# Four raw weight tiles loaded among the first attention blocks, converted beside the second to fifth, with every clamp on VectorE

## The chip, the cores and the metric

The kernel runs on one core of a Trainium2 chip. The metric is the device time of one launch in microseconds (us). The engines are TensorE (PE, matrix products into PSUM), VectorE (DVE), ScalarE (ACT), GpSimd (POOL) and SyncE (SP), which here issues all DMA transfers. Each engine works through its own list of instructions in order; semaphores tie the lists together.

## The reference

Everything is 32-bit floating point. Attention with two kinds of mask feeds a gated layer, and this feeds a layer that takes the largest of three products.

```python
batch, n_heads, seq, head_dim = (4, 8, 576, 64)
scores = scale * np.matmul(q, k.transpose(0, 1, 3, 2))
mask_local = (rel >= 0) & (rel < stride)                 # heads 0 to 3, stride 32
mask_strided = (rel >= 0) & (pos[None, :] % stride == pos[:, None] % stride)   # heads 4 to 7
...                                                      # softmax over the last axis
x = np.ascontiguousarray(attn_out.transpose(0, 2, 1, 3)).reshape(B * S, H * D)   # 2304 x 512
g = x @ w_gate                                           # 512 x 1536
silu = g * (1.0 / (1.0 + np.exp(-g)))
x = silu * (x @ w_val) @ w_out                           # 512 x 1536, then 1536 x 512
h = np.maximum(np.maximum(x @ w1, x @ w2), x @ w3)       # 512 x 768 each
return h @ w_out2                                        # 768 x 512
```

The weights reach the core as 64-bit words (a tile of 128 x 512 weights is 512 KB) and are converted there.

## The kernel before

**Two halves.** In the first half, attention and the gated layer run together, over five chunks of at most 480 of the 2304 tokens (`ROWS`). For each chunk there are 12 slots, one for each 128 columns of the hidden layer: gate product and SiLU (`emit_gate`, L499), value product and multiplication by the SiLU (`emit_val`, L507; the multiplication is L511 on DVE), and output product one slot later (`emit_out`, L517). In the second half the three products of the last layer and their maximum run for three pairs of token blocks (`Group`, `out2`).

**Split numbers.** Each operand of a product is split into a high and a low part (`split`, L122: the high part is a copy on ACT, L126, the low part a subtraction on DVE or POOL, L129), and each product is three matmuls: high with high (L484), high with low (L485), low with high (L486).

**Weights.** `load` (L136) brings a raw tile of 64-bit words into one of four buffers (`raw_p`). `convert` (L141) turns it into 32-bit numbers: `q` from the low words (L149 on POOL for the first three tiles, else L151 on ACT), the absolute value of the high words (L152, ACT), a clamp of it (L154, DVE, but POOL for the first three tiles), then shift and mask (L156), merge of the sign (L157) and sum with `q` (L158), all on DVE. `split_w` (L161) splits the result. The order of the 36 tiles is gate 0, value 0, gate 1, value 1, output 0, gate 2, value 2, output 1 and so on (L686). In the first chunk the kernel makes three weight steps in each slot (L716: load up to three tiles ahead, convert one, split one); before it stand eight such steps (`LEADW`).

**Early attention.** The first chunk can't begin before its part of `x` is there. Eight blocks (four strided ones, four local ones, each a pair of units) are loaded ahead of all else, in order (L730); after the blocks whose number is in `RAW_AT` one raw weight tile is put into the queue. The loop at L735 then runs scores (L286, PE), masked maximum (L294, DVE), exponentials (L299, ACT), normalization (L304), transposes (L309) and their copy (L312 or L314), the product with V (L323) and the split into `xh` and `xl` (L328 ACT, L329 DVE); the last three run four blocks later than the first ones. In this loop `step_cvt()` converts weight tiles.

**Order on the engines.** The program is written in one order and a scheduler, with a cost model of its own, makes the order on each engine from it when the kernel is built. The attention of the other chunks is made in pieces (`fill`, L772) in the slots of the chunk before; it uses L397 and L419 (POOL products), L400 and L422 (DVE sums) and more local blocks. The conversion of the second half's weights is tied to the slots from the second chunk on (L774 to L781).

Of the kernel before, what the change touches and what calls it, by code (L numbers as in the profile page):

```python
# [12 lines left out]
ALU = mybir.AluOpType  # L13
# [32 lines left out]

NRING = 4
SEAM = 9
RAW_AT = [2, 7]
SCALE = 1.0 / D ** 0.5  # L50
MASKED = -1.0e9 / SCALE

W_MIN = 2.0 ** -15
W_MAX = 122879.9921875
# [3 lines left out]
def tile_attention_swiglu_maxout(  # L58
# [11 lines left out]
    nc = tc.nc  # L70
# [29 lines left out]
    def f32(ap):  # L100
        return ap.bitcast(F32)
# [39 lines left out]
    def convert(key):  # L141

        raw = raws.pop(key)
        hi, lo = raw[:, :, 1], raw[:, :, 0]
        q = wpool.tile([128, 512], I32, name="q", tag="w")
        w = wpool.tile([128, 512], I32, name="w32", tag="w")

        if n_cvt[0] < 3 and key[0] in ("g", "v", "o"):
            nc.gpsimd.tensor_scalar(q, lo.bitcast(U32), 2.0 ** -29, 1.0, ALU.mult, ALU.mult)  # L149
        else:  # L150
            nc.scalar.activation(q, lo.bitcast(U32), AF.Copy, scale=2.0 ** -29)  # L151
        nc.scalar.activation(f32(w), f32(hi), AF.Abs)  # L152
        eng = nc.gpsimd if key[0] in ("g", "v", "o") and n_cvt[0] < 3 else nc.vector
        eng.tensor_scalar(f32(w), f32(w), W_MIN, W_MAX, ALU.max, ALU.min)  # L154

        nc.vector.tensor_scalar(w, w, 3, 0x3FFFFFFF, ALU.logical_shift_left, ALU.bitwise_and)  # L156
        nc.vector.scalar_tensor_tensor(w, hi, -0x40000000, w, ALU.bitwise_and, ALU.bitwise_or)  # L157
        nc.vector.tensor_tensor(w, w, q, ALU.add)  # L158
        cvt[key] = f32(w)
# [171 lines left out]
    def local_block(g, early=False):  # L331


        def dst(src):
            for c, i0, i1, o in pieces(LR * g[0], LR * (g[-1] + 1)):
                t, w = slice(i0 * STRIDE, i1 * STRIDE), slice(o * STRIDE, (o + i1 - i0) * STRIDE)
                xh, xl = x_tile(c)
                yield xh[:, 0:2, t], xl[:, 0:2, t], src[:, :, w]

        return Block(loc[g[0]:g[-1] + 1], KB, [mask[0 if n % (NI // LR) == 0 else 1] for n in g], dst, early)  # L340

    def strided_block(srcs, b, g, early=False):

        _, rows, nr = ON_PE[b]

        def dst(src):
            for u, n in enumerate(g):
                r0 = min(n * nr, STRIDE - nr)
                su = src[:, :, u * QB:u * QB + nr * rows].rearrange("p a (r i) -> p a r i", i=rows)
                for c, i0, i1, o in pieces(b * NI, b * NI + rows):  # L350
                    def part(t):
                        t = t[:, 2:4, :width(c)].rearrange("p a (i r) -> p a r i", r=STRIDE)
                        return t[:, :, r0:r0 + nr, i0:i1]

                    xh, xl = x_tile(c)
                    yield part(xh), part(xl), su[:, :, :, o:o + i1 - i0]

        return Block(srcs[g[0]:g[-1] + 1], rows * nr, [smask[b]] * len(g), dst, early)

    def pairs(ns):  # L360
        ns = list(ns)
        return [ns[i:i + 2] for i in range(0, len(ns), 2)]
# [329 lines left out]
    n_load, n_cvt, n_split = [0], [0], [0]  # L692
# [6 lines left out]
    def step_load(upto):  # L699
        while n_load[0] < min(upto, limit[0]):  # L700
            key = order[n_load[0]]
            load(key, source(key))
            n_load[0] += 1
# [12 lines left out]
    def weight_step():  # L716
        step_load(n_cvt[0] + AHEAD)
        step_cvt()
        step_split(nc.gpsimd)
# [6 lines left out]
    if True:  # L726
        blocks = [strided_block(st0, 0, g, True) for g in pairs(range(st0.shape[0]))]
        blocks += [local_block(g, True) for g in pairs(range(EARLY))]
        nc.sync.dma_start(cst, shape_consts)
        for i, blk in enumerate(blocks):  # L730
            blk.load()
            if i in RAW_AT:
                step_load(n_load[0] + 1)
        lag = 4
        for i in range(len(blocks) + lag):  # L735
            if i < len(blocks):
                blocks[i].scores()
                blocks[i].softmax(nc.gpsimd if i % 3 == 2 else nc.vector)
            if len(blocks) - 2 <= i < len(blocks):
                step_cvt()  # L740
            if i >= lag:
                blocks[i - lag].transpose(nc.vector if i % 3 == 2 else nc.scalar)
                blocks[i - lag].pv()
        step_split(nc.gpsimd)
        step_split(nc.gpsimd)
        step_load(n_cvt[0] + 2)
        step_cvt()
        for k in range(LEADW):
            weight_step()
        pending = None  # L750
        slots = [(c, f) for c in range(NC) for f in range(NF)]
        fill = {}
        for c in range(1, NC):
            for i, st in enumerate(attention_steps(c)):
                fill.setdefault(i if c == 1 else (c - 1) * NF + i - 3, []).extend(st)
        later = [step for g in range(NFP) for i in range(3) for step in pair_steps(i, g)]
        later += [step for f in range(NF2) for step in wo2_steps(f)]
        due, done = 0.0, 0
        for s, (c, f) in enumerate(slots):
            work = c == 0  # L760
            if c > 0:
                reload("v", f)
                reload("o", f)
            if work:
                weight_step()
            t = emit_gate(c, f)
            if work:
                weight_step()
            emit_val(c, f, t)
            if work:  # L770
                weight_step()
            for step in fill.get(s, []):  # L772
                step()
            if c > 0:  # L774
                due += PACE[c]
                with ExitStack() as tied:
                    for ins in last_val:
                        tied.enter_context(tc.issue_after(ins))
                    while later and done < int(due):
                        later.pop(0)()  # L780
                        done += 1  # L781
            if (c, f) == (NC - 1, SEAM):
                assert not later
                attn.close()
                two = ctx.enter_context(ExitStack())
                y_p, yr0_p = (sub(two, n, 1, side="right", reuse_waits="tile") for n in ("y", "yr0"))
                ring0_p = sub(two, "ring0", 1, side="right", reuse_waits="tile")
                yr_p = [yr0_p]
                ring_p = [ring0_p]
                y = [split_y(load_y(0, k)) for k in range(2)]  # L790
                load_w(0, 0, 0)
            if pending is not None:
                emit_out(*pending)
            pending = (c, f)
        emit_out(*pending)
# [130 lines left out]
```

## Time and profile before

| | before |
|---|---|
| median of three runs | 881.88 us (879.77 to 882.62) |
| profiled execution | 881.39 us, of which span 879.6 us |
| PE busy | 820.3 us (93%) |
| DVE busy | 555.9 us (63%) |
| ACT busy | 384.0 us (44%) |
| POOL busy | 382.3 us (43%) |

The span is what the trace covers, from the first instruction to the last. Shares are means over stages that are limited by different things; in 40 slices of 22 us each, in tenths, the page gives:

```text
PE   5789879898999989999998889999999999999997
DVE  2988999967757598668768943433545254433441
```

PE is the engine that works nearly all the time in the later slices, DVE in slices two to eight (22 to 176 us).

### The profile page before, as it was taken

Reading aid. Unit: us, or ns where it says so; the run is one execution under the profiler, and the core shown is the slowest. Engines: PE = TensorE matmul, PEld = TensorE weight load, DVE = VectorE, ACT = ScalarE, POOL = GpSimd, SP = SyncE. Lnnn points to the kernel's source line nnn. Section 1 sums busy time; section 2 is a strip of 40 time slices with the busy share of each in tenths; the row PEclk is TensorE's granted clock in tenths of the full one; section 3 lists DMA queues with packets and bytes.
Section 4 is the critical chain, followed back from the end, with each engine's and each line's share of the span. In section 5 each row is a group of like instructions: output and inputs, shape, how many; then the busy total and the mean of one; then the engine's idle time right before and its main releaser. Section 6 shows DMA issues by size and latency. Waiting matters only on the chain.

```text
span 879.6 us, 12559 instructions
## 1 busy us (share of the span) xinstructions
PE 820.3 (93%) x4376; PEld 731.7 (83%) x4376; DVE 555.9 (63%) x1097; ACT 384.0 (44%) x857; POOL 382.3 (43%) x301
## 2 busy tenths in 40 slices
PE   5789879898999989999998889999999999999997
PEld 5677658687788878999897779989999899989986
DVE  2988999967757598668768943433545254433441
ACT  4778586734445454364634233432335123422221
POOL 0443654474757676667596632430213021211110
PEclk9789789999999999999999989999999999999999
DMA  9868757896695759869676687578856476453601
GB/s 234 244 219 289 235 187 260 320 366 189 209 330 192 245 190 312 275 207 319 208 249 234 224 268 225 189 245 342 330 217 213 182 251 245 175 215 118 241 1 72
DMA packets 81774, 203.76 MB, mean 232 GB/s; under 512 B 9484, under 2 KB 50224, under 8 KB 78128
## 3 DMA queue, kind: packets, MB, share of 16 engines
q1 hardware_dynamic: 81712, 202.97, 68.1%
q8 instruction: 35, 0.57, 0.2%
q14 instruction: 27, 0.22, 0.1%
HBM read 161.26 MB, written 41.68 MB: 231 GB/s over the span
## 4 chain that ended last, share of the span: by engine, by line
PE 49%; DVE 10%; DMA 4%; ACT 4%; issue 3%; POOL 2%; SPq 0%; DVEq 0%; ACTq 0%; POOLq 0%
PE ps_a L585 13%; PE ps_z L658 8%; PE ps_c L585 6%; PE ps_b L585 3%; PE ps_v L484 2%; PE ps_g L484 2%; PE ps_v L485 2%; PE ps_v L486 2%; PE ps_g L486 2%; PE ps_g L485 2%; PE ps_y L484 2%; PE ps_y L486 2%; PE ps_y L485 2%; DVE w L156 2%; DMA w_v<-wvdr 1%
## 5 line engine op out<-in xcount | busy, mean ns | idle before, releaser
L129 POOL TENSOR_TENSOR hl<-t,hh 128x384 fp32r<-128x384 f32 x36 | 37.6, 1048 | 208.5 <-ACT hh L126 167.2
L484 PE MATMUL ps_g<-xh,wh_g 128*128 128x448 f32 (+1 forms) x240 | 94.4, 393 | 10.4 <-ACT ht L504 8.1
L129 POOL TENSOR_TENSOR hl<-ht,hh 128x448 fp32r<-128x448 f32 (+1 forms) x60 | 75.5, 1258 | 60.5 <-ACT hh L126 58.8
L419 POOL TENSOR_TENSOR pr<-stv,stsc 128x1088 f32<-128x1088 f32 (+17 forms) x44 | 75.2, 1710 | 58.1 <-DVE sto L422 35.9
L486 PE MATMUL ps_v<-xh,w_v 128*128 128x448 f32 (+1 forms) x240 | 91.5, 381 | 8.2 <-DVE w_v L129 8.2
L484 PE MATMUL ps_v<-xh,w_v 128*128 128x448 f32 (+1 forms) x240 | 92.4, 385 | 4.4 <-ACT w_v L126 2.4
L585 PE MATMUL ps_a<-yhT,wr 128*128 128x384 f32 x324 | 94.4, 338 | 0.6 <-ACT s L599 0.6
L486 PE MATMUL ps_g<-xh,wl_g 128*128 128x448 f32 (+1 forms) x240 | 92.7, 386 | 1.3 <-POOL wl_g L129 1.3
L485 PE MATMUL ps_g<-xl,wh_g 128*128 128x448 f32 (+1 forms) x240 | 92.4, 385 | 0.0
L485 PE MATMUL ps_v<-xl,w_v 128*128 128x448 f32 (+1 forms) x240 | 91.1, 379 | 0.0
L485 PE MATMUL ps_y<-hl,w_o 128*128 128x448 f32 (+1 forms) x240 | 89.2, 376 | 1.0 <-POOL hl L129 1.0
L397 POOL TENSOR_TENSOR pr<-stk,stq 128x1088 f32<-128x1088 f32 (+17 forms) x44 | 76.9, 1747 | 30.1 <-DVE stsc L400 23.2
L486 PE MATMUL ps_y<-hh,w_o 128*128 128x448 f32 (+1 forms) x240 | 86.4, 377 | 2.3 <-POOL w_o L129 2.3
L484 PE MATMUL ps_y<-hh,w_o 128*128 128x448 f32 (+1 forms) x240 | 86.2, 380 | 0.2 <-ACT w_o L126 0.2
L599 ACT ACTIVATE s<-ps_a 128x384 f32<-128x384 f32 x81 | 39.4, 490 | 98.4 <-PE ps_a L585 98.1
L126 ACT ACTIVATE hh<-ht 128x448 fp32r<-128x448 f32 (+1 forms) x60 | 35.2, 587 | 106.0 <-DVE ht L511 105.6
L658 PE MATMUL ps_z<-wo2t,hh 128*128 128x512 f32 x216 | 64.8, 392 | 0.9 <-ACT osb L667 0.7
L484 PEld LDWEIGHTS ps_g<-xh,wh_g 128*128 128x128 f32 x240 | 47.2, 197 | 19.1 <-ACT ht L504 10.5
L511 DVE TENSOR_TENSOR ht<-ps_v,ht 128x448 f32<-128x448 f32 (+1 forms) x60 | 37.8, 630 | 37.9 <-PE ps_v L486 26.6
L585 PEld LDWEIGHTS ps_a<-yhT,wr 128*128 128x128 f32 x324 | 59.7, 188 | 1.7 <-ACT s L599 1.1
L486 PEld LDWEIGHTS ps_v<-xh,w_v 128*128 128x128 f32 x240 | 46.1, 192 | 15.1 <-DVE w_v L129 10.3
L484 PEld LDWEIGHTS ps_v<-xh,w_v 128*128 128x128 f32 x240 | 46.2, 192 | 11.1 <-DVE ht L511 3.4
(134 smaller groups left out, 1971.5 us busy)
## 6 DMA issues: line engine op xcount, KB each, us to landing
wr<-wsdr SPq DMA_DIRECT2D x27, 1792.0 KB, 7.2
raw<-in_w_dram SPq DMA_DIRECT2D x60, 512.0 KB, 4.8
w_v<-wvdr SPq DMA_DIRECT2D x48, 512.0 KB, 5.0
w_o<-wodr SPq DMA_DIRECT2D x48, 512.0 KB, 4.9
wsdr<-whi SPq DMA_DIRECT2D x27, 256.0 KB, 3.3
wvdr<-w_v SPq DMA_DIRECT2D x12, 512.0 KB, 4.1
wodr<-w_o SPq DMA_DIRECT2D x12, 512.0 KB, 5.2
loct<-in_loc_dram SPq DMA_DIRECT2D x24, 192.0 KB, 6.5
```

What stands on the lines that cost most here:

```text
L126: a = nc.scalar.activation(hi, src, AF.Copy)
L129: return a.ins, lo_eng.tensor_tensor(lo, src, f32(hi), ALU.subtract).ins
L156: nc.vector.tensor_scalar(w, w, 3, 0x3FFFFFFF, ALU.logical_shift_left, ALU.bitwise_and)
L397: eng.tensor_tensor(pv, self.k[:, 0:i + 1, :], self.q[:, r:r + 1, :].to_broadcast([128, i + 1, D]), ALU.mult)
L419: eng.tensor_tensor(pv, self.v[:, :, 0:i + 1], self.sc[:, r:r + 1, 0:i + 1].to_broadcast([128, D, i + 1]), ALU.mult)
L484: nc.tensor.matmul(ps, wh, xh, start=first, stop=False)
L485: nc.tensor.matmul(ps, wh, xl, start=False, stop=False)
L486: nc.tensor.matmul(ps, wl, xh, start=False, stop=last)
L511: m = nc.vector.tensor_tensor(t, ps[:, :n], t, ALU.mult).ins
L585: nc.tensor.matmul(ps, wts[:, c, a, ks], y[k][b], start=first and k == q == 0, stop=k == 1 and q == 2, skip_group_check=True,)
L599: nc.scalar.activation(s, self.a, AF.Copy)
L658: nc.tensor.matmul(z[j], a[:, ts], w[:, f, b], start=f == q == 0, stop=f == NF2 - 1 and q == 2)
```

## The change

Four raw tiles instead of two go into the queue among the eight blocks' loads: after the blocks 0, 1, 3 and 5 instead of 2 and 7. The early loop converts four tiles, in its steps 1 to 4, instead of two in its steps 6 and 7. After the loop nothing else is taken out, so that the program then stands two conversions further on. The clamp of the first three tiles moves from POOL to DVE; their `q` stays on POOL.

```diff
-RAW_AT = [2, 7]
+RAW_AT = [0, 1, 3, 5]
...
-        eng = nc.gpsimd if key[0] in ("g", "v", "o") and n_cvt[0] < 3 else nc.vector
-        eng.tensor_scalar(f32(w), f32(w), W_MIN, W_MAX, ALU.max, ALU.min)
+        nc.vector.tensor_scalar(f32(w), f32(w), W_MIN, W_MAX, ALU.max, ALU.min)
...
                 blocks[i].scores()
                 blocks[i].softmax(nc.gpsimd if i % 3 == 2 else nc.vector)
-            if len(blocks) - 2 <= i < len(blocks):
+            if 1 <= i < 5:
                 step_cvt()
```

Since one line is gone, every line behind it has a number lower by one in the changed kernel (L152 stays, L156 becomes L155, L312 becomes L311).

The order on ACT at the program's start, before: exponentials of the first four blocks (`sme`, 128x64), copy of the first transposed block (`qe`), exponentials of the fifth (128x96), and the first absolute value of a raw tile (`w_384` is gate 0).

```order
L299 ACT_TABLE_LOAD
L299 ACTIVATE sme,state<-sme,state 128x64 x16
L312 ACTIVATE qe<-ps_a 64x512
L299 ACTIVATE sme,state<-sme,state 128x96 x4
L328 ACTIVATE xh<-ps_a 128x2x4x15
L299 ACTIVATE sme,state<-sme,state 128x96 x4
L328 ACTIVATE xh<-ps_a 128x2x4
L152 ACTIVATE w_384<-raw 128x512
```

The same place now (`w_253`, `w_278`, `w_303` and `w_328` are gate 0, value 0, gate 1 and value 1).

```order
L152 ACTIVATE w_253<-raw 128x512
L298 ACTIVATE sme,state<-sme,state 128x64 x4
L152 ACTIVATE w_278<-raw 128x512
L298 ACTIVATE sme,state<-sme,state 128x64 x4
L152 ACTIVATE w_303<-raw 128x512
L298 ACTIVATE sme,state<-sme,state 128x64 x8
L151 ACTIVATE q<-raw 128x512
L152 ACTIVATE w_328<-raw 128x512
L311 ACTIVATE qe<-ps_a 64x512
L298 ACTIVATE sme,state<-sme,state 128x96 x4
```

The work on the four raw tiles now stands in front of the exponentials of the first, the second and the third block and of the copy of the first transposed block; before, the first of it stood behind the exponentials of the sixth block.

The order on DVE before, at the last piece of `xl` that the first gate product needs (128x2x96; `w_545` and `w_557` are gate 1 and value 1).

```order
L329 TENSOR_TENSOR xl<-ps_a,xh 128x2x128
L329 TENSOR_TENSOR xl<-ps_a,xh 128x2x4
L157 SCALAR_TENSOR_TENSOR w_545<-raw,w_545 128x512
L157 SCALAR_TENSOR_TENSOR w_557<-raw,w_557 128x512
L329 TENSOR_TENSOR xl<-ps_a,xh 128x2x96
```

The same place now (`w_591`, `w_605` and `w_619` are value 2, output 1 and gate 3, the seventh to ninth tile; the last row is the last piece of `xl` of the first chunk).

```order
L155 TENSOR_SCALAR w_605<-w_605 128x512
L153 TENSOR_SCALAR w_619<-w_619 128x512
L328 TENSOR_TENSOR xl<-ps_a,xh 128x2x128
L328 TENSOR_TENSOR xl<-ps_a,xh 128x2x96
L156 SCALAR_TENSOR_TENSOR w_591<-raw,w_591 128x512
L156 SCALAR_TENSOR_TENSOR w_605<-raw,w_605 128x512
L301 TENSOR_SCALAR stat<-stat 128x4
L155 TENSOR_SCALAR w_619<-w_619 128x512
L328 TENSOR_TENSOR xl<-ps_a,xh 128x2x4x15
```

The first gate product's last input now stands behind work on the ninth weight tile; before, behind work on the fourth.

## Rows read from the trace of the kernel before

**Rows 1.** Busy time by stage: us, then PE, PEld, DVE, ACT, POOL, granted clock, DMA.

```profile
0.00:52.10 52.10, 35.32 (x272) 30.93 (x272) 32.96 (x162) 32.67 (x125) 14.70 (x17) 0.90 0.81 225
52.10:156.30 104.20, 92.38 (x467) 74.79 (x467) 100.93 (x187) 74.44 (x154) 52.77 (x35) 0.90 0.75 245
156.30:179.30 23.00, 19.44 (x102) 15.42 (x102) 22.86 (x38) 15.40 (x31) 11.86 (x10) 0.93 0.92 335
179.30:245.00 65.70, 60.97 (x335) 50.79 (x334) 46.73 (x91) 27.14 (x66) 45.81 (x33) 0.97 0.74 255
19.99:40.63 20.64, 15.73 (x190) 13.41 (x190) 19.03 (x87) 16.15 (x64) 11.00 (x9) 0.86 0.92 257
24.75:41.90 17.15, 12.25 (x140) 10.60 (x141) 16.27 (x63) 12.46 (x49) 9.73 (x7) 0.79 0.80 236
```

**Rows 2.** PE's waits from 42 to 220 us: total, times, longest.

```profile
PE ps_v L486 <- DVE w_v L129: 8.2, 6, 2.9
PE ps_a L309 <- POOL sm L304: 3.2, 2, 2.4
```

**Rows 3.** DVE's groups from 80 to 180 us.

```profile
L157 DVE SCALAR_TENSOR_TENSOR w<-raw,w 128x512 int32<-128x512 int32 x23 | 22.8, 990 | 0.1
L158 DVE CUSTOM_DVE_ANT_0 w<-w,q 128x1024 uint16<-128x1024 uint16 x23 | 20.6, 896 | 0.1
L154 DVE TENSOR_SCALAR w<-w 128x512 f32<-128x512 f32 x23 | 16.5, 719 | 0.0
L156 DVE TENSOR_SCALAR w<-w 128x512 int32<-128x512 int32 x23 | 15.7, 685 | 0.2
```

**Rows 4.** PE's order of time: scores of blocks 2, 3 and 5; first gate product.

```profile
9.98 1.97 PE L286 MATMUL ps_a<-ke,qe 128*128 128x64 f32 x8 [0.94 <-DMA ke<-in_st_dram]
14.76 1.94 PE L286 MATMUL ps_a<-ke,qe 128*128 128x64 f32 x8 [2.81 <-DMA ke<-in_st_dram]
...
19.74 1.71 PE L286 MATMUL ps_a<-ke,qe 128*128 128x96 f32 x8
...
41.91 0.75 PE L484 MATMUL ps_g<-xh,wh_g 128*128 128x480 f32 x1
```

**Rows 5.** What the DMA engines moved from 0 to 24 and to 30 us.

```profile
DMA packets 6092, 5.71 MB, mean 238 GB/s; under 512 B 414, under 2 KB 5902, under 8 KB 6092
...
DMA packets 7181, 7.69 MB, mean 256 GB/s; under 512 B 500, under 2 KB 6667, under 8 KB 7178
```

**Rows 6.** ACT's order of time: copy of the first block, two weight instructions.

```profile
19.99 0.59 ACT L312 ACTIVATE qe<-ps_a 64x512 f32<-64x512 f32 x1 [0.84 <-PE ps_a L309]
...
58.39 0.66 ACT L151 ACTIVATE q<-raw 128x512 int32<-128x512 uint32 x1
58.95 0.66 ACT L152 ACTIVATE w<-raw 128x512 f32<-128x512 f32 x1
```

**Rows 7.** DVE's order of time: weight instructions, three of the multiplications L511.

```profile
50.08 0.42 DVE L154 TENSOR_SCALAR w<-w 128x512 f32<-128x512 f32 x1
50.42 0.68 DVE L158 CUSTOM_DVE_ANT_0 w<-w,q 128x1024 uint16<-128x1024 uint16 x1
51.02 0.42 DVE L154 TENSOR_SCALAR w<-w 128x512 f32<-128x512 f32 x1
...
52.10 0.66 DVE L511 TENSOR_TENSOR ht<-ps_v,ht 128x480 f32<-128x480 f32 x1 [0.33 <-ACT ht L504]
...
156.33 0.66 DVE L511 TENSOR_TENSOR ht<-ps_v,ht 128x480 f32<-128x480 f32 x1
...
179.34 0.66 DVE L511 TENSOR_TENSOR ht<-ps_v,ht 128x480 f32<-128x480 f32 x1
```

**Rows 8.** Order of time: POOL's second clamp; DVE's normalization alone and beside it.

```profile
29.46 2.24 POOL L154 TENSOR_SCALAR w<-w 128x512 f32<-128x512 f32 x1
...
23.82 0.55 DVE L304 TENSOR_TENSOR sme<-sme,state 128x384 f32<-128x384 f32 x1
29.85 0.96 DVE L304 TENSOR_TENSOR sme<-sme,state 128x384 f32<-128x384 f32 x1
```

## The prediction

> **What bounds the kernel now.** I read the table of stages first [rows 1]. The reader is to see two stages that are limited by different engines. From 52.10 to 156.30 us DVE works 100.93 of 104.20 us, PE only 92.38, and PE's granted clock is 0.90 there: it is the engine that waits. From 179.30 to 245 us PE works 60.97 of 65.70 us and DVE 46.73. Then the waits of PE [rows 2]: the largest item is the split of a value weight (8.2 us), so PE is kept waiting by converted weights. Then DVE's groups in the full stretch [rows 3]: 23 conversions cost 22.8 + 20.6 + 16.5 + 15.7 = 75.6 us in 100 us, 3.29 us for one (the groups overlap a little at their ends). So the first chunk goes at the speed at which DVE converts weights. Ahead of it lies a third stage: up to 52.10 us DVE works 32.96 us and is idle for 19.1 [rows 1], because the first blocks' data come in one after another [rows 4].
>
> The change wants to use that idle time. What it can bring is at most what DVE is idle less than before until the conversions end, and only as far as PE can then make use of it.
>
> **What the change moves.** I counted, in the order of instructions on DVE, what stands in front of each multiplication L511 (one for each slot). In front of the first one there are 9 clamps, 6 shifts, 7 merges, 5 sums and 1 split more than before (ten tiles converted and not five). In front of the tenth the lead is 8, 5, 5, 6 and 2. In front of the twelfth all 36 tiles are done in both kernels, and only the three clamps taken from POOL remain. In front of the nineteenth these three are the whole difference. So nothing but these clamps is added, and nothing removed; the rest is a question of when.
>
> *Step 1, the loads.* The same transfers stand in the queue ahead of all others (eight blocks, four raw tiles, two further local blocks), but four raw tiles now stand among the blocks' loads and not one (the second one of before came behind the last block). Block 5 had one raw tile ahead of it and its scores began at 19.74 [rows 4]. A raw tile is 0.52 MB, and 7.69 MB in 30 us are 0.256 MB for each us [rows 5]: 2.05 us each. The pattern fits: block 3, behind the raw tile, came 4.78 us after block 2, and the two blocks after it took 4.98 together [rows 4]. The fourth raw tile is behind block 5 and three raw tiles more than before, so it lands at about 19.74 + 3 x 2.05 = 25.9. At the rate from 24 to 30 us (1.98 MB in 6 us, 0.33 MB for each us [rows 5]) it would be 24.5.
>
> *Step 2, ACT.* ACT works in order, and the two instructions on this fourth tile stand in front of the copy of the first transposed block. That copy began at 19.99 [rows 6]; now it can't before 25.9 + 2 x 0.56 = 27.0 (0.56 is the distance of two weight instructions [rows 6]). From that copy to its last piece for the first chunk ACT worked 16.15 us [rows 1]. Of these, 7 were weight instructions, in the new order there are 15, and four exponentials of a later block come in between (0.36 each, estimated as a little more than half of a 0.66 us instruction): 16.15 + 8 x 0.56 + 1.45 = 22.1. ACT is then done at 49.1. The second route is DVE: the last block's scores lie at 24.75, they move by 3 x 2.05 to 30.9; DVE worked 16.27 us from there to the gate [rows 1], and about 3.0 us of weight and mask work come in between, net: 50.2. I take 49 for the first gate product, against 41.91 [rows 4]: PE starts 7 us later. Lower end 46 (faster loads, and ACT's waits that fall away), upper end 53 (the fifth to ninth raw tile also stand in front of the last pieces on ACT and DVE, and they wait for buffers).
>
> *Step 3, DVE to the first multiplication.* Distances of starts without POOL beside: 0.34 us for a clamp (a shift has the same form), 0.60 for a sum (a merge and a split the same) [rows 7]. The additional work is 15 x 0.34 + 13 x 0.60 = 12.9 us, so 45.9 busy. The multiplication came 10.2 us after the gate (52.10 - 41.91), so now at 59.2. DVE has idled 13.3 us by then, 5.8 fewer than before. The 12.9 us are hidden by that idle time; if they took half as much again beside POOL, it would still hold them.
>
> *Step 4, the conversions.* From the first to the tenth multiplication DVE was full: 104.2 us [rows 7]. The new order has 0.7 us less weight work there, so the tenth comes at 59.2 + 103.5 = 162.7, and not at 156.33. PE, which needed 92.38 us at clock 0.90 [rows 1], is not the bound there: it waits as before.
>
> *Step 5, the payback.* From the tenth to the twelfth it took 23.0 us, with DVE busy for 22.86 [rows 1]. Here 11.2 us of weight work are gone (10 x 0.34 + 13 x 0.60), so PE decides: 19.44 us busy at clock 0.93, less the 1.6 us that the lower clock cost (0.07 x 23.0), are 17.8. The twelfth multiplication comes at 180.5, and not at 179.34: 1.2 us later.
>
> *Step 6, after it.* The attention work for the second chunk is then a few sums further on. The wait that this can shorten is that of PE for a normalization on POOL, 3.2 us in all [rows 2]. Between nothing and all of it I take half: 1.6 us. Behind the nineteenth multiplication the order on DVE is the old one but for single neighbours.
>
> *The clamps.* On POOL one took up to 2.24 us, and the normalization on DVE beside it 0.96 instead of 0.55 us [rows 8]. Three clamps give back about three times 0.4, 1.2 us, and cost 3 x 0.34 on DVE: nothing, and both lie in front of the gate.
>
> The Trainium skill ("SBUF — State Buffer", section "SBUF: two separate sides") says more: DVE and GpSimd share one pair of ports, which is locked for a whole instruction, so that the loser stands still. By that rule the three clamps would have kept DVE for up to 6.7 us. The trace does not agree for this pair: the normalization ran beside the clamp and was 0.4 us slower.
>
> **Sum.** 881.39 (the profiled execution) + 1.2 - 1.6 = 881.0 us. The median of the runs is 0.5 us higher than the profiled execution; I forecast no change that can be measured. 0.3% is 2.6 us, about what a measurement of this kernel can tell from no change: under 879.2 is faster, over 884.5 slower.
>
> **Rivals.**
>
> *PE gets its weights earlier (faster).* For it: the weight waits of [rows 2] would vanish with a lead of five tiles, and idle DVE time is what it has most of in the first stage. Against it: L511 stands in the same queue as the conversions. With the gate at 46 and the 3.2 us gone entirely, the sum is 881.0 - 3 - 1.6 = 876.4.
>
> *The raw tiles hold up attention (slower).* ACT is the place: the absolute value of each raw tile waits for its landing, and the copies and exponentials of the blocks that have landed wait behind it. The price is the later gate, us for us, as long as DVE has nothing ready. With the gate at 53 and nothing regained in step 6 it is 881.0 + 4 + 1.6 = 886.6. It decides from a gate at about 51 (nothing regained) or 52.5 (half). For it: ACT's order, and DMA engines that were fully busy already. Against it: ACT worked only 16.15 of 20.64 us in its stretch and can make up for some.
>
> *The clamps on POOL had DVE stand still.* Places like [rows 8], but with the whole 2.24 us lost three times: DVE would gain 6.7 - 1.2 = 5.5 us before the gate, and the sum would be 875.5. Beside it stands the rule quoted above from the Trainium skill; the 0.96 us speak against it.
>
> **How the numbers follow.** No measurable change 0.39, PE's weights earlier 0.29, attention held up 0.27, the lock 0.05. Faster is 0.29 + 0.05 = 0.34, same 0.39, slower 0.27. The likeliest case's own range is 879.2 to 884.5. The range for 8 in 10 reaches to both other cases, with some 2 us beyond 876.4 and 1.4 beyond 886.6 for contention in the 104 us of step 4: 874 to 888.
>
> **What would show it.** Steps 1 and 2: the copy of the first transposed block at about 27 us behind a wait for a raw tile, and the first gate product between 46 and 53. Step 3: the first L511 at about 59, with ten conversions done. Step 4: the tenth at about 163, DVE without gaps, PE still waiting for weights. Step 5: the slots ten to twelve in about 9 us each, without waits for weights. The prediction is wrong if the gate comes near 42 all the same, if DVE has gaps for missing raw tiles after the gate, or if conversions run faster than 3.29 us in the full stretch.

## The result, and the profile after

| | before | after |
|---|---|---|
| median of five runs each | 881.57 us (879.77 to 882.62) | 887.21 us (886.49 to 890.69) |
| ratio after / before | | 1.0081 (95% interval 1.0061 to 1.0101) |
| profiled execution, span in it | 881.39, 879.6 us | 887.2, 885.4 us |

The kernel became 0.8% slower, clear of the noise. I had forecast 881.0 us and no measurable change; 887.21 lies inside the wide range of 874 to 888, near the size that the second rival had given (886.6, but for a gate at 53).

The first view is the table of stages after the change (us, busy time of PE, PEld, DVE, ACT and POOL, granted clock, DMA share, GB/s), cut at the first, tenth and twelfth multiplication (now L510), as [rows 1] were; its last row runs from ACT's first copy to the first gate product.

```profile
0.00:62.57 62.57, 43.28 (x306) 36.26 (x306) 47.15 (x190) 43.77 (x144) 15.19 (x18) 0.84 0.83 259
62.57:168.70 106.13, 85.54 (x429) 70.77 (x425) 104.42 (x175) 67.13 (x136) 57.22 (x36) 0.90 0.77 261
168.70:184.37 15.67, 15.67 (x70) 13.46 (x69) 8.57 (x21) 7.43 (x17) 14.41 (x9) 0.89 0.61 207
184.37:250.00 65.63, 62.95 (x362) 52.89 (x361) 39.66 (x102) 34.80 (x79) 35.57 (x30) 0.97 0.70 228
22.82:46.25 23.43, 17.66 (x184) 14.93 (x184) 21.14 (x94) 20.02 (x71) 5.60 (x5) 0.70 0.86 267
```

The conversions end earlier, as meant: from the tenth to the twelfth multiplication DVE is only 8.57 of 15.67 us busy and PE has no gap. But the first multiplication comes at 62.57 and not at 52.10, and the twelfth at 184.37 and not at 179.34 [rows 7]. ("Multiplication" is the one by the SiLU on DVE, one for each slot; "gate", with a time, is the start of the first gate product on PE.)

PE's waits from 42 to 220 us after the change (total, times, longest), against [rows 2]:

```profile
PE ps_g L483 <- ACT ht L503: 8.9, 3, 5.3
PE ps_v L483 <- DVE ht L510: 6.6, 3, 5.4
PE ps_a L322 <- issue: 4.5, 1, 4.5
PE ps_a L322 <- ACT loct L311: 1.8, 2, 1.2
PE ps_g L484 <- DVE xl L328: 1.4, 2, 1.2
PE ps_g L483 <- ACT xh L327: 1.4, 2, 1.0
PE ps_a L308 <- POOL sm L303: 0.9, 1, 0.9
```

Every wait for a weight is gone, the 8.2 us for the value weights among them, and the wait for the normalization fell from 3.2 to 0.9 us. In their place stand 15.5 us of waiting for `ht`, which the SiLU on ACT and the multiplication on DVE write. In the largest wait for DVE, 5.4 us up to 122.64, the multiplication stood behind conversions without a gap. In the largest for ACT, 5.3 us up to 93.64, the SiLU stood behind four exponentials, which had waited 3.80 us for DVE, and two instructions on a raw tile. Before, all waits for weights together were 15.3 us in this stretch, those for `ht` 2.5. The sum of all waits listed rose from 21.0 to 25.5 us.

How the start moved: PE's order of time at the scores of the last early block and the first two gate products; [rows 4] has the gate of before at 41.91.

```profile
26.19 1.03 PE L285 MATMUL ps_a<-ke,qe 128*128 128x96 f32 x8
...
46.26 0.77 PE L483 MATMUL ps_g<-xh,wh_g 128*128 128x480 f32 x1 [0.43 <-ACT xh L327]
48.19 0.77 PE L484 MATMUL ps_g<-xl,wh_g 128*128 128x480 f32 x1 [1.16 <-DVE xl L328]
```

The last early block's scores lay at 24.75 before, so the raw tiles moved them by only 1.4 us. The gate moved by 4.35 us, and its second product waits once more for DVE. What lies between shows on ACT (start, duration, operation, in brackets the idle time ahead of it):

```profile
21.67 0.68 ACT L151 ACTIVATE q<-raw 128x512 int32<-128x512 uint32 x1 [1.63 <-DMA raw<-in_w_dram]
...
22.82 0.58 ACT L311 ACTIVATE qe<-ps_a 64x512 f32<-64x512 f32 x1
...
34.63 0.69 ACT L151 ACTIVATE q<-raw 128x512 int32<-128x512 uint32 x1
...
38.47 0.64 ACT L311 ACTIVATE qe<-ps_a 96x512 f32<-96x512 f32 x1
38.95 0.73 ACT L151 ACTIVATE q<-raw 128x512 int32<-128x512 uint32 x1
...
43.77 0.66 ACT L152 ACTIVATE w<-raw 128x512 f32<-128x512 f32 x1
...
45.88 0.33 ACT L327 ACTIVATE xh<-ps_a 128x192 fp32r<-128x192 f32 x1 [0.47 <-PE ps_a L322]
```

Ten instructions on the fifth to ninth raw tile, about 5.6 us (0.56 each [rows 6]), stand between 34.63 and 44.43, in front of or among the copies and pieces of `xh` for which the gate waits. Before, three such instructions stood behind 32 us (33.76 to 35.55), and ACT then waited 2.27 us for PE.

Where the 5.8 us of the longer span went shows in the sums of two tables that run to the twenty-fourth multiplication (295.10 us before, 301.00 after; 1,436 and 1,441 matmul records). First before, then after:

```profile
sum 295.10, PE 256.85 PEld 212.85 DVE 235.22 ACT 177.53 POOL 155.31; mean PE 51.37 PEld 42.57 DVE 47.04 ACT 35.51 POOL 31.06
```
```profile
sum 301.00, PE 258.44 PEld 216.86 DVE 233.48 ACT 178.95 POOL 154.41; mean PE 51.69 PEld 43.37 DVE 46.70 ACT 35.79 POOL 30.88
```

PE is idle for 42.56 us and not 38.25 (+4.3) and needs 1.6 us more for nearly the same number of matmuls. From there on the distance hardly changes (+5.9 at the twenty-fourth multiplication, +5.8 at the end). Over the whole execution PE is busy for 820.2 us and was for 820.3, so at the end all of the difference is idle time.

### The profile page after: what moved, and what is told of

Read it like the earlier page. It is cut to its first block, busy times and chain, and to the rows that moved or that the text cites. A ratio compares the mean times of both kernels' runs of the same rounds, so it can differ in the third digit from the quotient of the medians.

```text
span 885.4 us, 12556 instructions
## 1 busy us (share of the span) xinstructions
PE 820.2 (93%) x4376; PEld 735.1 (83%) x4376; DVE 554.2 (63%) x1100; ACT 383.2 (43%) x855; POOL 378.9 (43%) x298
## 4 chain that ended last, share of the span: by engine, by line
PE 55%; DVE 15%; DMA 5%; issue 5%; ACT 4%; POOL 3%; SPq 1%; DVEq 0%; ACTq 0%; POOLq 0%
PE ps_a L584 13%; PE ps_z L657 8%; PE ps_c L584 6%; PE ps_b L584 3%; PE ps_g L483 3%; PE ps_v L483 3%; PE ps_g L484 2%; PE ps_g L485 2%; PE ps_v L485 2%; PE ps_y L484 2%; PE ps_y L483 2%; PE ps_y L485 2%; PE ps_v L484 2%; DVE w L155 2%; DVE w L156 2%
## 5 line engine op out<-in xcount | busy, mean ns | idle before, releaser
L129 POOL TENSOR_TENSOR hl<-ht,hh 128x448 fp32r<-128x448 f32 (+1 forms) x60 | 77.8, 1297 | 74.5 <-ACT hh L126 72.9
L418 POOL TENSOR_TENSOR pr<-stv,stsc 128x1088 f32<-128x1088 f32 (+17 forms) x44 | 72.7, 1651 | 57.5 <-DVE sto L421 41.6
L396 POOL TENSOR_TENSOR pr<-stk,stq 128x1088 f32<-128x1088 f32 (+17 forms) x44 | 77.8, 1768 | 37.5 <-DVE stsc L399 29.5
L484 PE MATMUL ps_y<-hl,w_o 128*128 128x448 f32 (+1 forms) x240 | 91.1, 379 | 0.7 <-POOL hl L129 0.7
L485 PE MATMUL ps_y<-hh,w_o 128*128 128x448 f32 (+1 forms) x240 | 90.6, 377 | 0.0
L483 PE MATMUL ps_y<-hh,w_o 128*128 128x448 f32 (+1 forms) x240 | 87.1, 380 | 0.0
L510 DVE TENSOR_TENSOR ht<-ps_v,ht 128x448 f32<-128x448 f32 (+1 forms) x60 | 37.9, 631 | 47.4 <-PE ps_v L485 37.6
L483 PEld LDWEIGHTS ps_v<-xh,w_v 128*128 128x128 f32 x240 | 46.2, 192 | 16.6 <-DVE ht L510 11.6
L503 ACT ACTIVATE ht<-ps_g 128x448 f32<-128x448 f32 (+1 forms) x60 | 33.3, 554 | 52.3 <-PE ps_g L485 38.4
## 6 DMA issues: line engine op xcount, KB each, us to landing
wsdr<-whi SPq DMA_DIRECT2D x27, 256.0 KB, 3.3
```

Source lines behind the costliest of these rows:

```text
L129: return a.ins, lo_eng.tensor_tensor(lo, src, f32(hi), ALU.subtract).ins
L396: eng.tensor_tensor(pv, self.k[:, 0:i + 1, :], self.q[:, r:r + 1, :].to_broadcast([128, i + 1, D]), ALU.mult)
L418: eng.tensor_tensor(pv, self.v[:, :, 0:i + 1], self.sc[:, r:r + 1, 0:i + 1].to_broadcast([128, D, i + 1]), ALU.mult)
L483: nc.tensor.matmul(ps, wh, xh, start=first, stop=False)
L484: nc.tensor.matmul(ps, wh, xl, start=False, stop=False)
L485: nc.tensor.matmul(ps, wl, xh, start=False, stop=last)
```

## The experiments

Theory G (the gate): PE starts late because weight work stands in front of the attention's last pieces on ACT and DVE, and a late start isn't given back. Rival Q (the queue): the multiplications stand behind ten conversions and not five, and these waits for `ht` are the loss. All ratios are to the kernel before, run beside each kernel on the same chip (its median was 879.94 to 881.59 there, so compare ratios, not medians); "lead" is the number of conversions finished on DVE ahead of the first multiplication.

| kernel | edit of | lead | gate, us | median, us | ratio (95%) |
|---|---|---|---|---|---|
| before | | 5 | 41.91 | 881.57 | 1 |
| changed | before | 10 | 46.26 | 887.21 | 1.0081 (1.0061 to 1.0101) |
| clamps_alone | before | 8 | 48.00 | 885.81 | 1.0054 (1.0037 to 1.0072) |
| loads_alone | before | 5 | 43.20 | 887.67 | 1.0058 (1.0037 to 1.0079) |
| changed_short_lead | changed | 7 | 47.54 | 889.95 | 1.0089 (1.0064 to 1.0113) |
| before_long_lead | before | 10 | 41.09 | 883.19 | 1.0022 (1.0009 to 1.0035) |
| changed_rest_deferred | changed | 5 | 41.73 | 883.79 | 1.0032 (1.0014 to 1.0049) |
| before_rest_deferred | before | 3 | 40.63 | 883.49 | 1.0043 (1.0025 to 1.0061) |
| before_late_gate | before | 9 | 49.70 | 899.39 | 1.0216 (1.0195 to 1.0237) |
| changed_clamps_on_pool | changed | 12 | 56.03 | 891.81 | 1.0125 (1.0097 to 1.0152) |
| changed_later_conversions | changed | 9 | 50.05 | 891.16 | 1.0120 (1.0097 to 1.0143) |
| before_raw_tile_thrice | before | 8 | 49.32 | 888.79 | 1.0090 (1.0069 to 1.0112) |
| changed_rest_deferred_long_lead | changed | 10 | 40.40 | 880.62 | 1.0008 (0.9986 to 1.0030) |

**The parts alone.** clamps_alone, the clamps of the kernel before on VectorE:

```diff
-        eng = nc.gpsimd if key[0] in ("g", "v", "o") and n_cvt[0] < 3 else nc.vector
+        eng = nc.vector
```

> Kernel before with the three clamps on VectorE and nothing else. In the built order 8 conversions (before: 5, changed kernel: 10) now stand in front of the first multiplication L511 on VectorE. Theory Q (the loss comes from multiplications that stand in VectorE's queue behind conversions that nobody needs yet): the first L511 about 4 to 6 us later than 52.1 us, total 883 to 886 us. Theory G (the loss is the later first gate product, 46.3 and not 41.9 us): gate unchanged near 42 us, total 881 to 882.5 us.

loads_alone, the places of the raw tiles alone:

```diff
-RAW_AT = [2, 7]
+RAW_AT = [0, 1, 3, 5]
```

> Kernel before with the four raw tiles loaded after blocks 0, 1, 3 and 5, and the conversions and clamps as before. 5 conversions stand in front of the first L511, as before. Theory Q: the first gate product comes later by the loads (44 to 46 us), the first L511 follows about 10 us after it, total 881 to 883.5 us, since the conversions end at the same time as before. Theory G: total later by as much as the gate, 885 to 887 us.

changed_clamps_on_pool, the changed kernel with the clamps where they were:

```diff
-        nc.vector.tensor_scalar(f32(w), f32(w), W_MIN, W_MAX, ALU.max, ALU.min)
+        eng = nc.gpsimd if key[0] in ("g", "v", "o") and n_cvt[0] < 3 else nc.vector
+        eng.tensor_scalar(f32(w), f32(w), W_MIN, W_MAX, ALU.max, ALU.min)
```

> Changed kernel with the first three clamps back on GpSimd. In the built order 9 conversions stand in front of the last piece of xl (6 in the changed kernel) and 12 in front of the first L511. Theory gate: gate at 47 to 50 us, total 887 to 890 us. Rival lead: total 881 to 885 us.

Each part alone costs over half of the loss, so they don't add up: each makes the scheduler write another order. clamps_alone took a time that I had expected by rival Q, but its gate moved too, against what I had expected, so it doesn't tell the two apart. loads_alone lost about what G had said for a gate at 44 to 46, but its gate came at 43.20. PE's order of time in clamps_alone, where no load was moved:

```profile
48.00 0.77 PE L484 MATMUL ps_g<-xh,wh_g 128*128 128x480 f32 x1 [0.96 <-ACT xh L328]
```

Its gate is 6.1 us later than before, with eight conversions in front of the first multiplication instead of five. Three instructions that I had priced at nothing set another order on all engines. With the clamps back on POOL the changed kernel is slower still (1.0125; the intervals just touch), with the gate at 56.03: in the changed order VectorE seems the better place. That run also shows a limit of G: its gate is 14.1 us later than before, its twelfth multiplication 9.7 (189.00), its twenty-fourth 7.2 (302.31), and its end 11.0 by the median (0.0125 x 881): with twelve conversions done ahead, part was given back.

**The queue.** In changed_short_lead, the eight weight steps ahead of the slots are left to the slots, and those of each slot are tied behind the multiplication of the slot before:

```diff
-LEADW = 8
+LEADW = 0
...
+    def tied_step():
+        with ExitStack() as tied:
+            if last_val:
+                tied.enter_context(tc.issue_after(last_val[0]))
+            weight_step()
...
-                weight_step()
+                tied_step()
```

> Changed kernel with the eight leading weight steps left to the slots (LEADW 0) and each slot's weight steps on VectorE queued behind the multiplication of the slot before. 7 conversions stand in front of the first L511 and not 10, 8 and not 13 in front of the second, 33 and not 36 in front of the tenth; gate as in the changed kernel (46 us). Theory Q: first L511 at 57 to 59 us and not 62.6, total 881 to 884 us. Theory G: total 886 to 888 us, as the changed kernel.

before_long_lead puts the multiplication of slot f of the first chunk behind conversion 10 + 3f on DVE in the kernel before (`sums` collects the last instruction of each conversion):

```diff
-        m = nc.vector.tensor_tensor(t, ps[:, :n], t, ALU.mult).ins
+        with ExitStack() as behind:
+            if c == 0:
+                behind.enter_context(tc.issue_after(sums[min(10 + 3 * f, 36) - 1]))
+            m = nc.vector.tensor_tensor(t, ps[:, :n], t, ALU.mult).ins
```

> Kernel before with each multiplication of the first chunk queued on VectorE behind as many conversions as in the changed kernel (10, 13, 16 and so on); loads, early conversions and clamps as before, gate near 42 us. Theory Q: first L511 at 60 to 64 us, total 884 to 888 us. Theory G: total 881 to 882.5 us.

DVE's order of time in before_long_lead at the sixth and the twenty-fourth multiplication, and PE's two largest waits for `ht` there from 42 to 220 us:

```profile
133.03 0.65 DVE L515 TENSOR_TENSOR ht<-ps_v,ht 128x480 f32<-128x480 f32 x1
...
295.29 0.65 DVE L515 TENSOR_TENSOR ht<-ps_v,ht 128x480 f32<-128x480 f32 x1
```
```profile
PE ps_v L485 <- ACT ht L505: 10.4, 4, 4.0
...
PE ps_g L485 <- DVE ht L515: 4.2, 4, 1.4
```

The sixth multiplication came at 107.36 before: it is 25.7 us late here, PE waits for `ht` as in the changed kernel, and at the twenty-fourth 0.2 us are left of it (295.07 before), though PE had some 20 matmuls fewer behind it there (1,415 records, 1,436 before). At the end 0.22% is left, 1.9 us (0.0022 x 881): most of the delay is given back, not all, and by itself Q doesn't reach 0.81%. changed_short_lead fits that: with three conversions fewer in front it isn't faster than the changed kernel. But its gate is 1.3 us later (47.54), so it is no clean test.

**The gate, undone.** changed_rest_deferred keeps the four loads, the four early conversions and the clamps, and lets only the weight work written behind the early loop begin, on ACT and on DVE, behind all early pieces of `xh` and `xl` (`parts` collects them in L327 and L328); before_rest_deferred is the same edit of the kernel before:

```diff
-        step_load(n_cvt[0] + 2)
-        step_cvt()
-        for k in range(LEADW):
-            weight_step()
+        with ExitStack() as behind:
+            for ins in parts:
+                behind.enter_context(tc.issue_after(ins))
+            step_load(n_cvt[0] + 2)
+            step_cvt()
+            for k in range(LEADW):
+                weight_step()
```

> Changed kernel with all conversions from the fifth on queued on ScalarE and VectorE behind the last pieces of x of the early blocks (4 conversions in front of the last piece of xl and not 6, 5 in front of the first L511 and not 10). Theory gate (the time of the first gate product passes to the end us for us; the stretch from it to the 24th L511 was 252 to 258 us in six kernels, whatever was converted ahead): gate at 42 to 44 us, total 882 to 884 us. Rival lead (a conversion that is done before the gate shortens the stretch behind it by 2 to 3 us): the earlier gate is given back, total 886 to 888 us.

> Kernel before with all conversions from the third on queued behind the last pieces of x of the early blocks (3 conversions in front of the first L511 and not 5). Theory gate: gate at 39 to 41 us, total 879 to 881 us. Rival lead: total 882 to 885 us, since two conversions less are done when the gate starts.

ACT in changed_rest_deferred, as far as it differs from the rows of the changed kernel above:

```profile
34.90 0.59 ACT L312 ACTIVATE qe<-ps_a 96x512 f32<-96x512 f32 x1 [0.23 <-PE ps_a L309]
...
36.97 0.59 ACT L312 ACTIVATE qe<-ps_a 96x512 f32<-96x512 f32 x1 [0.56 <-PE ps_a L309]
...
40.47 0.80 ACT L328 ACTIVATE xh<-ps_a 128x256 fp32r<-128x256 f32 x2 [0.30 <-PE ps_a L323]
...
42.97 0.65 ACT L152 ACTIVATE q<-raw 128x512 int32<-128x512 uint32 x1
```

Up to 31 us ACT does the same as in the changed kernel, 0.2 us later. Then the copy and the pieces run without the weight work, which begins at 42.97, and the gate is at 41.73. So the weight work that the scheduler pulled in from behind the loop delays the gate; the loads, the four early conversions and the clamps together do so by about 1 us at most (the same edit of the kernel before has its gate at 40.63). 0.0049 of the 0.0081 go away, and the interval lies outside the changed kernel's; 0.0032 are left although the gate is as early as before. before_rest_deferred goes against G: its gate is 1.3 us earlier than before, and it is 0.43% slower, as the rival in its expectation had said. Its lead is 3, and PE waits 7.7 us for `wh_g` and 5.9 for `w_v` there: a lead can also be too short.

**The gate, delayed.** before_late_gate queues the last block's pieces of `xl` behind the sixth conversion:

```diff
-LEADW = 8
+LEADW = 5
...
-                blocks[i - lag].pv()
+                with ExitStack() as behind:
+                    if i == len(blocks) + lag - 1:
+                        while n_cvt[0] < 6:
+                            step_load(n_cvt[0] + 3)
+                            step_cvt()
+                        behind.enter_context(tc.issue_after(sums[5]))
+                    blocks[i - lag].pv()
```

> Kernel before, loads and clamps as before, but the last early block's pieces of xl on VectorE are queued behind the sixth conversion (9 conversions in front of the first L511, 12 in front of the second, much as in the changed kernel). Theory gate: gate at 46 to 48 us, total 886 to 888 us. Rival lead: total 880 to 883 us, since the conversions done ahead pay for the later gate.

before_raw_tile_thrice loads the first raw tile three times, and adds no computation:

```diff
-        raw_dma[0] = nc.sync.dma_start(raw.rearrange("p a b -> p (a b)"), src.bitcast(I32))
+        for again in range(3 if key == ("g", 0) else 1):
+            raw_dma[0] = nc.sync.dma_start(raw.rearrange("p a b -> p (a b)"), src.bitcast(I32))
```

> The kernel before with its first raw tile loaded three times into the same buffer, which puts two more transfers of 0.52 MB in front of the fourth to eighth block and changes no computation. The theory that a late first gate product is passed on us for us: the gate comes about 4 us later (45 to 46), and the kernel takes 884.5 to 887 us (ratio 1.004 to 1.006). Rival, that the weight work which now fits in front of the gate is worth its time: gate 45 to 46 and yet 881 to 883 us (within 0.2%). A third, that any new order on the engines costs some us whatever the gate: 885 or more even with the gate under 44.

changed_later_conversions writes the four conversions in later steps of the early loop:

```diff
-            if 1 <= i < 5:
+            if 4 <= i < 8:
```

> The changed kernel with its four early conversions written in steps 4 to 7 of the early loop instead of 1 to 4; the four raw tiles are loaded where they are in the changed kernel, the clamps stay on VectorE. If the conversions' place in front of the attention work is what makes the first gate product late, it starts at 42 to 44 us instead of 46.3 and the kernel takes 883 to 885 us (ratio to before about 1.003). If the loads among the blocks alone make it late, the gate stays at 45 to 47 and the time at 887 (1.006 to 1.008). If only the lead of the weights counted (nine conversions in front of the first multiplication instead of ten), it is within 1 us of the changed kernel as well, whatever the gate does.

The gate products of before_raw_tile_thrice and, in the second fence, of changed_later_conversions:

```profile
49.32 0.77 PE L485 MATMUL ps_g<-xh,wh_g 128*128 128x480 f32 x1 [1.51 <-ACT xh L329]
```
```profile
50.05 0.75 PE L483 MATMUL ps_g<-xh,wh_g 128*128 128x480 f32 x1
```

In the first the gate is 7.4 us late, more than the 4 that two transfers should cost, and the kernel 7.9 us slower (0.0090 x 881), though its lead is eight conversions: us for us, and a little over. In the second my expectation of the gate was wrong (42 to 44): the scheduler pulled still more weight work in front, and the loss followed the gate, 1.2% at 50.05. In before_late_gate the twenty-fourth multiplication is 17.6 us late for a gate 7.8 us late, over twice what G says; the rest isn't explained. None of the three moves the gate and nothing else: the order on the engines changed with it, as the leads of eight and nine show.

**Both at once.** changed_rest_deferred_long_lead joins the edits of changed_rest_deferred and before_long_lead:

> The changed kernel with both edits that came closest to the kernel before: the weight work written behind the early loop stands behind the early pieces of xh and xl, and the multiplication of slot f of the first chunk stands on VectorE behind conversion 10 + 3f. If the gate decides (41 to 43 us) and the multiplications' place in the queue is free, 882 to 884 us, ratio 1.002 to 1.004, with the twelfth multiplication 5 to 9 us later than in the kernel before and the twenty-fourth within 2 us of it. If conversions in front and an early gate add up, it is faster than before: under 880 us. If the late multiplications cost here what the queue theory says, 888 or more.

PE's order of time there, at the last early block's scores and the gate:

```profile
29.51 1.86 PE L286 MATMUL ps_a<-ke,qe 128*128 128x96 f32 x8
...
40.40 0.46 PE L484 MATMUL ps_g<-xh,wh_g 128*128 128x480 f32 x1
```

The last block's scores are 4.8 us later than before, and the gate is still 1.5 us earlier: the late weight work doesn't stand in front, and PE's granted clock stayed at 1.00 from 32 to 42 us (0.64 before). The kernel has the changed kernel's loads, conversions, clamps and lead of ten, and no loss is left that can be measured (1.0008, interval around 1). Here the early conversions are harmless; they aren't worth anything that shows either, and no version that I ran beats the kernel before.

**What follows.** Of the thirteen kernels in the table the six with the gate at 43.2 us or earlier lie between 1 and 1.0058, the seven with the gate at 46.26 or later between 1.0054 and 1.0216. A straight line through all thirteen (least squares, ratio times 881 us over gate) rises by 0.8 us for each us of the gate, with a wide scatter: before_late_gate lies 9.5 us above it and changed_clamps_on_pool 3.8 below, and without before_late_gate the slope is 0.7. The stretch from the gate to the twenty-fourth multiplication says the same more plainly: it takes 251.6 to 256.0 us in nine of the thirteen, with gates from 40.40 to 50.05 and leads from 5 to 10. Outside are changed_clamps_on_pool (246.3, lead 12), loads_alone (257.8), before_rest_deferred (259.1, lead 3) and before_late_gate (263.0).

Q by itself falls. G holds for the larger part of the loss, not to the us: loads_alone loses 5.1 us (0.0058 x 881) with a gate only 1.3 us late (its second gate product, which waits 1.81 us for DVE, is 2.6 late), and before_rest_deferred 3.8 with an early one. What costs them the rest stays open; both have a lead of five or fewer and again wait for weights. A third rival, that any new order costs some us wherever the gate is, was not tested by itself: the five other orders with an early gate lose 0.08 to 0.58%.

## Why the prediction was wrong, step by step

*Step 1 (loads): wrong in size.* The fourth raw tile had landed at 21.67 and not 25.9, and the last block's scores moved by 1.4 us and not 6.2. I had priced each tile at a full rate's 2.05 us; but the queue had room. In the first 20 us the DMA engines moved 232 GB/s before and 274 after.

*Step 2 (ACT, gate): in range, by another route.* The copy came at 22.82 (27.0 forecast), the path from there to the gate took 23.4 us (22.1, but as work; ACT was busy for 20.02 of it), the gate 46.26 (49, range 46 to 53). Not the landing of the raw tiles held the gate up; the weight work on the fifth to ninth tile, which I had named as a risk of the upper end, was the main cause, by changed_rest_deferred.

*Step 3 (first multiplication): failed.* I carried the 10.2 us between gate and multiplication over from the trace of before, and let DVE's idle time ahead of the gate hide all of the added work. They became 16.3. The stretch from the gate to the multiplication, first before, then after, and after that the SiLU for which the multiplication had waited before, and the multiplication itself:

```profile
41.91:52.10 10.19, 7.74 (x34) 6.43 (x33) 8.01 (x25) 9.44 (x28) 3.36 (x3) 0.83 0.53 170
```
```profile
46.26:62.57 16.31, 12.78 (x66) 9.64 (x66) 16.31 (x34) 13.68 (x37) 7.30 (x5) 0.80 0.61 215
```
```profile
56.75 0.57 ACT L503 ACTIVATE ht<-ps_g 128x480 f32<-128x480 f32 x1
...
62.57 0.64 DVE L510 TENSOR_TENSOR ht<-ps_v,ht 128x480 f32<-128x480 f32 x1
```

DVE has no gap there: of its 14.2 us of added work ahead of the multiplication (47.15 - 32.96) 8.3 fell behind the gate (16.31 - 8.01), and 5.9 in front of it. The SiLU was done at 57.32, 11.1 us after the gate (10.2 before); the other 5.2 us the multiplication stood behind conversions. So the overlap that I had assumed did not happen. The multiplication came at 62.57 (59.2). DVE idled 15.4 us by then (13.3) and worked 47.15 (45.9).

*Step 4 (conversions): too short.* From the first to the tenth it took 106.1 us (103.5). The groups from 80 to 180 us, against [rows 3]:

```profile
L157 DVE CUSTOM_DVE_ANT_0 w<-w,q 128x1024 uint16<-128x1024 uint16 x20 | 23.1, 1156 | 0.0
L156 DVE SCALAR_TENSOR_TENSOR w<-raw,w 128x512 int32<-128x512 int32 x20 | 18.4, 923 | 0.2
L153 DVE TENSOR_SCALAR w<-w 128x512 f32<-128x512 f32 x19 | 15.1, 797 | 1.4 <-ACT w L152 1.4
L155 DVE TENSOR_SCALAR w<-w 128x512 int32<-128x512 int32 x20 | 14.6, 729 | 0.0
```

One conversion now costs 1.156 + 0.923 + 0.797 + 0.729 = 3.60 us, not 3.29. I had put the work on POOL at nothing here. From 80 to 180 us POOL is busy for 57.15 us and not 53.57, its long products for the attention (L396) came seven times and not three (17.3 us and 8.6), and a merge on DVE (L156) beside one of them, in the second line, took 3.02 us:

```profile
84.35 2.98 POOL L396 TENSOR_TENSOR pr<-stk,stq 128x1088 f32<-128x1088 f32 x1
```
```profile
84.86 3.02 DVE L156 SCALAR_TENSOR_TENSOR w<-raw,w 128x512 int32<-128x512 int32 x1
```

That points to POOL; no run separates it.

*Step 5 (payback): larger than forecast, in part by luck.* 15.7 us from the tenth to the twelfth multiplication (17.8), without a gap on PE, as I had said. But it was so short because PE had less to do in it (70 matmul records, 102 before) and not because the clock rose (0.89, 0.93 before). And it started from too far behind: +5.0 us at the twelfth and not +1.2. The errors add up: 3.4 (step 3) + 2.6 (step 4) - 2.1 (step 5) = 3.9, and 1.2 + 3.9 is 5.1, the +5.0 measured but for rounding.

*Step 6 (after it): nothing came.* The normalization's wait did shrink, by 2.3 us, but the distance grew from +5.0 to +5.8 and not to -0.4.

*Clamps: right by themselves, wrong in the sum.* Their own time is as small as I said; clamps_alone lost 4.8 us (0.0054 x 881) through the new order.

So the step that failed is step 3, with what hangs on it: I priced a gate 7 us late at +1.2 us by the twelfth multiplication and at no more behind it, because DVE's idle time was to hide the added work and the later steps to give the rest back. Measured, a gate 4.35 us late stood at +5.0 there and at +5.8 at the end. DVE was indeed full from the first to the tenth multiplication (104.42 of 106.13 us); what was wrong is that a late gate drowns in that. The runs show: with the weight work behind the gate's inputs 0.0049 of the 0.0081 are gone (changed_rest_deferred), with the multiplications held back as well no loss is left (changed_rest_deferred_long_lead), and late multiplications alone cost 0.0022 (before_long_lead). That PE mostly doesn't get back what it misses at the start is my reading of all thirteen together; changed_clamps_on_pool got part of it back.

The rival with the held-up attention had the right size by luck: its 886.6 were for a gate at 53, and by its own terms it would not have decided below 51; the gate came at 46.26, and through weight work, not the landing of raw tiles. "Weights earlier" fell: all weight waits went, and waits for `ht` of the same size came.

## What to carry to other kernels

When work is prefetched into idle time at the start, look first at what it stands in front of on each in-order queue, and price the start of the engine that is busy to the end: here a start 4.4 us later went with 5.8 us at the end, while a delay of up to 26 us in a middle stage cost 1.9. A wait that vanishes from the list of waits is no gain until the sum of all waits is smaller: here 15.3 us of waits for weights went and the sum still rose by 4.5. Where a scheduler sets the order, an edit of three small instructions can move the start by 6 us, so read its order before pricing, and tie prefetched work behind the critical inputs.

## What the runs showed of the hardware

**PE's clock falls at the start, and stays down longer where the gate is late.** Tables by 10 us (columns as above) of the kernel before and after:

```profile
22.00:32.00 10.00, 8.01 (x116) 6.34 (x114) 9.18 (x47) 8.73 (x41) 6.31 (x6) 1.00 1.08 304
32.00:42.00 10.00, 7.08 (x69) 6.63 (x69) 9.81 (x33) 5.55 (x17) 3.62 (x3) 0.64 0.61 180
42.00:52.00 10.00, 7.65 (x33) 6.34 (x32) 8.01 (x25) 9.25 (x28) 3.36 (x3) 0.84 0.52 170
```
```profile
22.00:32.00 10.00, 6.21 (x80) 4.96 (x80) 9.92 (x49) 8.24 (x36) 2.98 (x3) 1.00 1.11 298
32.00:42.00 10.00, 8.16 (x69) 6.77 (x69) 8.55 (x29) 9.43 (x29) 1.27 (x1) 0.51 0.71 267
42.00:52.00 10.00, 8.18 (x49) 6.33 (x50) 9.25 (x34) 8.32 (x31) 3.44 (x2) 0.50 0.59 195
```

After the change PE was busy for 6.21 of the 10 us ahead of the fall, with gaps for ACT's copies, and then ran at the lower level (0.50, which is 1.2 GHz) for the next 20 us; matmuls of 480 columns followed each other at 0.40 us up to 52.56, and at 0.22 from 53.08 on. The 240 matmuls ahead of the gate were busy for 30.50 us and not 27.58 (241), so part of the late gate may be the clock; no run separates them. changed_rest_deferred_long_lead, 9.49 us busy from 22 to 32, kept 1.00 until 42; before_raw_tile_thrice, busy for all 10 us there but for only 4.89 of the next ten, fell to 0.79 in these and to 0.50 from 42 to 52. From 42 to 52 the granted clock was 0.84 to 1.00 in the six kernels with the gate at 43.2 or earlier, and 0.50 to 0.54 in six of the seven with a later one (0.98 in changed_clamps_on_pool, which had 0.50 from 52 to 62).

**DVE and POOL did block each other.** In the prediction I had given this little weight, by one pair of instructions. After the change DVE's order of time has, and below it POOL's:

```profile
53.19 0.92 DVE L153 TENSOR_SCALAR w<-w 128x512 f32<-128x512 f32 x1
...
54.11 1.71 DVE L129 TENSOR_TENSOR w_v<-w,w_v 128x512 fp32r<-128x512 f32 x1
...
58.05 1.78 DVE L156 SCALAR_TENSOR_TENSOR w<-raw,w 128x512 int32<-128x512 int32 x1
```
```profile
52.58 1.25 POOL L303 TENSOR_TENSOR sm<-sm,stat 128x384 f32<-128x384 f32 x1 [2.08 <-DVE stat L301]
53.80 1.48 POOL L129 TENSOR_TENSOR w_o<-w,w_o 128x512 fp32r<-128x512 f32 x1
...
57.97 1.32 POOL L129 TENSOR_TENSOR wl_g<-w,wh_g 128x512 fp32r<-128x512 f32 x1 [0.79 <-POOL sm L303]
```

POOL's three instructions end at 53.83, 55.28 and 59.29, the three on DVE at 54.11, 55.82 and 59.83: 0.28, 0.54 and 0.54 us later, whenever they began; alone they take 0.42, 0.68 and 0.68. That is how it looks when DVE stands still until POOL is through. This agrees with the rule of the Trainium skill that the prediction had quoted ("SBUF — State Buffer", section "SBUF: two separate sides"), by which one of the two engines stands still for the whole instruction of the other, at these three places; the 0.96 us of [rows 8] do not show it. The trace of before holds one of either kind more: a merge on DVE at 28.94 ends at 29.92, 0.55 us behind POOL's `q` (28.48 to 29.37), and beside the third clamp on POOL (34.53 to 36.45) a sum on DVE takes its usual 0.68 us. The pair in step 4 looks the same: POOL ends at 87.33, DVE at 87.88. Whether such meetings make up the 0.31 us by which a conversion became dearer was not counted.
